# Splitting every pair of hidden chunks: low parts of 1+elu on GpSimd, an excess taken from each output tile, middle results in SBUF

## The chip, the cores and the metric

The kernel runs on one core of one Trainium2 chip. The metric is the device time of one execution in microseconds; before the change it is 1710.24 us, the median of three runs (1710.19 to 1712.89). The engines are called as the profile calls them: PE (TensorE), with PEld for its weight loads, DVE (VectorE), ACT (ScalarE), POOL (GpSimd) and SP (SyncE, which here issues DMAs). PE writes its results to PSUM; the other tiles lie in SBUF. L680 is line 680 of the kernel before.

## The reference

```python
def mab(q, kv):
    s = scale * (q @ kv.transpose(0, 2, 1))
    s = s - s.max(-1, keepdims=True)
    a = np.exp(s)
    a /= a.sum(-1, keepdims=True) + 1e-09
    return a @ kv
h = mab(I, x)                  # I: 32 inducing points, x: (4, 12480, 128)
attn = mab(x, h)               # (4, 12480, 128)

h = attn.reshape(49920, 128) @ w_in             # w_in: (128, 2048)
g = np.where(h > 0, h, np.exp(np.minimum(h, 0.0)) - 1.0)     # elu
out = g @ w_out                                 # w_out: (2048, 128)
```

Two attentions through 32 inducing points, then a feed-forward layer with 2048 hidden values per token and elu between its two products. Nearly all the work is the feed-forward layer. The weights are handed over as 64-bit floats, which the kernel takes apart itself; everything else is 32-bit.

## The kernel before

**Tiles.** The 12480 tokens of a batch are cut into 25 blocks, 15 of 512 tokens and 10 of 480, so there are 100 blocks (60 and 40) in four batches. The 2048 hidden values are 16 chunks of 128, taken two at a time: 8 pairs per block, 800 pairs in all. A tile of a pair is 128 partitions by 2 x 512 (or 2 x 480) values. Output stays transposed on the chip: a block's output tile is 128 output features by its tokens in one PSUM bank (`po`, two banks in turn), accumulated over all 8 pairs, and turned by DVE's transpose in squares of 32 by 32 (L688) before four DMAs on SP write it out.

**First product.** The second attention's weights a (32 per token) are not multiplied with h and then with w_in. h is multiplied with w_in once per batch (`project_h`), and the 32 rows of the result are stacked in a 128-row operand `hw` as high, low and high part and a block of ones; the attention weights are stacked for each block (`stk`) as high, high, low, and 1/32. One matmul per chunk (L618) in the type fp32r then gives ph = 1 + (attn @ w_in): the products of the parts, and the last 32 rows the one.

**One pair.** With ph = 1 + z in PSUM, four steps make the operands of the second product:

- `ffn_in` (L612): two matmuls into ph (three buffers `ph` of two banks), then ACT writes e = exp(ph - 1) into SBUF (L626, five buffers).
- `ffn_mid` (L629): DVE takes min(max(ph, 1), e), which is 1 + elu(z). For D pairs it goes back into ph in PSUM, for others into e in SBUF (L632).
- `ffn_split` (L636): for P and D pairs ACT writes gh, which is the value less one, rounded to fp32r (L641, four buffers).
- `ffn_low` (L643): what the rounding left, gl (four buffers). For D pairs DVE takes (ph - 1) - gh in one instruction (L648). For P and N pairs POOL first takes one from e in place (L653); for P pairs it then takes e - gh (L658).

The plan "PDNPDPND" (L28) says how each of the 8 pairs of a block is treated: three P, three D, two N. `ffn_out` (L660) does the second product into po (L680): for an N pair two matmuls in full 32-bit floats with the unsplit weights `wo_n`, which the profile shows as four instructions; for a split pair six matmuls in fp32r, gh with the high part `wo_h` of the weights, gh with their low part `wo_l`, and gl with `wo_h`, for each of two chunks.

**Order.** The order of the instructions on PE, DVE and ACT is written out by hand (L829 to L857). In round n come: the first product and exponential of pair n, the middle step and split of pair n-1, the low part of pair n-2, pieces of side work that have come due, and the second product of pair n-5 (LAG, L85; less at the beginning). So ACT's order is exponential n, split n-1; DVE's is middle step n-1, D low part n-2. Each engine takes its instructions in that order. POOL and SP are ordered by the framework.

**Side work.** The attention of later blocks and the next batch's first attention are cut into steps with due times (`attend` L699, `first_half` L707) and put between the pairs: scores on PE (L312, L531), transposes and reductions on DVE (L259, L394, L541, L549, L562, L579), exponentials on ACT, and on POOL the subtraction of the maximum (L550), the multiplication by the reciprocal sum (L570) and a low part (L591). The first batch's attention and the taking apart of the weights come before and among the first 13 pairs, in the hand-written order FIRST (L35): letters A to E are the stages of eight pieces of weights. L198, L202 and L208 are DVE's instructions in them, L212 and `split_w_out` (L230 to L239) make the final weights on POOL and ACT.

Of the kernel before, what the change touches and what calls it, by code (L numbers as in the profile page):

```python
# [9 lines left out]
F32 = mybir.dt.float32  # L10
F32R = mybir.dt.float32r
I32 = mybir.dt.int32
U32 = mybir.dt.uint32
AF = mybir.ActivationFunctionType
ALU = mybir.AluOpType
AX = mybir.AxisListType

P = 128
Q = 32
TM = 512  # L20
# [4 lines left out]

PLAN = "PDNPDPND"  # L28

# [13 lines left out]
def kernel(  # L45
# [8 lines left out]
    nc = tc.nc  # L54
    B, N, C = x.shape
# [18 lines left out]
    NFC = F // P  # L74
    NCP = NFC // 2
    assert len(PLAN) == NCP
    CHUNKS_S = [f for f in range(NFC) if PLAN[f // 2] != "N"]
    CHUNKS_N = [f for f in range(NFC) if PLAN[f // 2] == "N"]
    WHERE_S = {f: i for i, f in enumerate(CHUNKS_S)}
    WHERE_N = {f: i for i, f in enumerate(CHUNKS_N)}  # L80
    NSPLIT = len(CHUNKS_S)
    SCALE = 1.0 / math.sqrt(C)
    EPS = 1e-9

# [8 lines left out]
    const = ctx.enter_context(tc.tile_pool(name="const", bufs=1))  # L93
# [4 lines left out]
    ep = ctx.enter_context(tc.tile_pool(name="ep", bufs=2))  # L98
# [5 lines left out]
    ghp = ctx.enter_context(tc.tile_pool(name="ghp", bufs=GHB))  # L104
    glp = ctx.enter_context(tc.tile_pool(name="glp", bufs=GLB))
    op = ctx.enter_context(tc.tile_pool(name="op", bufs=2))
# [8 lines left out]
    def bank(name, take=False):  # L115
        if not steady and not take:
            return ps_h.tile([P, 2, 512], F32, tag="ph", name=name)[:, 0]
        t = ps_o.tile([P, 512], F32, tag=f"po{turn[0] % 2}", name=name)
        if take:
            turn[0] += 1  # L120
        return t
# [6 lines left out]
        out=fold, in_=ident.rearrange("p (c m) -> p m c", m=Q), axis=AX.X, op=ALU.add  # L128
    )
    sel4 = const.tile([P, 4, Q], F32, name="sel4")  # L130
    for c in range(4):
# [6 lines left out]
        out=mine, in_=ident.rearrange("p (c m) -> p c m", m=Q), axis=AX.X, op=ALU.add  # L138
# [5 lines left out]
    ps = bank("ps_ind")  # L144
# [3 lines left out]


    win_sb = const.tile([C, F], F32, name="win_sb")  # L150
    wo_n = const.tile([P, len(CHUNKS_N), C], F32, name="wo_n")
    wo_h = const.tile([P, NSPLIT, C], F32R, name="wo_h")
    wo_l = const.tile([P, NSPLIT, C], F32R, name="wo_l")
    WS = 512
    rebias = const.tile([P, 1], F32, name="rebias")
    nc.gpsimd.memset(rebias, -896.0)
# [73 lines left out]
    def split_w_out(s, w):  # L230
        for i in range(WC):
            f = s * WC + i
            t = w.low[:, i * C : (i + 1) * C]
            if f in WHERE_N:
                nc.scalar.copy(wo_n[:, WHERE_N[f], :], t)
            if f in WHERE_S:
                n = WHERE_S[f]
                nc.scalar.copy(wo_h[:, n, :], t)  # L238
                nc.gpsimd.tensor_sub(wo_l[:, n, :], t, wo_h[:, n, :].bitcast(F32))  # L239


    xT = {}
# [363 lines left out]
    live = {}  # L606

    def plan(n):
        b, k, cp = units[n]
        return PLAN[cp]  # L610

# [16 lines left out]

    def ffn_mid(n):  # L629
        v = live[n]  # L630
        v["g"] = v["ph"] if plan(n) == "D" else v["e"]
        nc.vector.scalar_tensor_tensor(  # L632
            out=v["g"], in0=v["ph"], scalar=1.0, in1=v["e"], op0=ALU.max, op1=ALU.min
        )

    def ffn_split(n):  # L636
        v, how = live[n], plan(n)
        shape = list(v["e"].shape)
        if how != "N":
            v["gh"] = ghp.tile(shape, F32R, tag="gh", name=f"gh_{n}")  # L640
            nc.scalar.activation(v["gh"], v["g"], AF.Copy, bias=-1.0)  # L641

    def ffn_low(n):  # L643
        v, how = live[n], plan(n)
        shape = list(v["e"].shape)
        if how == "D":
            v["gl"] = glp.tile(shape, F32R, tag="gl", name=f"gl_{n}")
            nc.vector.scalar_tensor_tensor(  # L648
                out=v["gl"], in0=v["g"], scalar=-1.0, in1=v["gh"].bitcast(F32),
                op0=ALU.add, op1=ALU.subtract,  # L650
            )
        else:
            nc.gpsimd.tensor_scalar(  # L653
                out=v["e"], in0=v["e"], scalar1=-1.0, scalar2=1.0, op0=ALU.add, op1=ALU.mult
            )
        if how == "P":
            v["gl"] = glp.tile(shape, F32R, tag="gl", name=f"gl_{n}")
            nc.gpsimd.tensor_sub(v["gl"], v["e"], v["gh"].bitcast(F32))  # L658

    def ffn_out(n):  # L660
        b, k, cp = units[n]
        v, how = live.pop(n), plan(n)
        T = BLOCKS[k][1]
        U = T // Q
        if cp == 0:
            outs[b, k] = bank(f"po_{b}_{k}", take=True)
        po = outs[b, k]
        parts = []
        for i in range(2):
            f = 2 * cp + i  # L670
            if how == "N":
                parts.append((0, wo_n[:, WHERE_N[f], :], v["e"][:, i]))
            else:
                w = WHERE_S[f]
                parts.append((1, wo_h[:, w, :], v["gh"][:, i]))
                parts.append((1, wo_l[:, w, :], v["gh"][:, i]))
                parts.append((2, wo_h[:, w, :], v["gl"][:, i]))
        parts.sort(key=lambda v: v[0])
        for i, (_, w, g) in enumerate(parts):
            nc.tensor.matmul(  # L680
                po[:, :T], w, g,
                start=(cp == 0 and i == 0),
                stop=(cp == NCP - 1 and i == len(parts) - 1),
            )
        if cp == NCP - 1:
            yield 1
            o = op.tile([P, U, Q], F32, tag="o", name=f"o_{b}_{k}")
            nc.vector.transpose(o.rearrange("p u d -> p (u d)"), po[:, :T])  # L688
            at = b * N + BLOCKS[k][0]
            dst = out[at : at + T, :]  # L690
            for dq in range(4):
                nc.sync.dma_start(
                    dst[:, dq * Q : (dq + 1) * Q].rearrange("(u t) d -> t u d", t=Q),
                    o[dq * Q : (dq + 1) * Q, :, :],
                )
# [45 lines left out]
    def first_batch(b):  # L741
# [32 lines left out]
        for s, w in enumerate(win + [w for w, _ in wout]):  # L774
            steps[f"A{s}"], steps[f"C{s}"] = w.take_apart, w.put_together
            steps[f"B{s}"] = lambda w=w, s=s: w.scale_of(s >= 6)
            if s < len(win):
                steps[f"D{s}"] = lambda w=w, s=s: w.finish(win_sb[:, s * WS : (s + 1) * WS])
            else:
                steps[f"D{s}"] = w.finish  # L780
                steps[f"E{s}"] = lambda w=w, s=s: split_w_out(s - len(win), w)
# [47 lines left out]
    for n, (b, k, cp) in enumerate(units):  # L829
        ffn_in(n)  # L830
        if n >= 1:
            ffn_mid(n - 1)
            ffn_split(n - 1)
        if n >= 2:
            ffn_low(n - 2)
        for r in list(running):
            go_on(r, n)
        while rest and rest[0][0] != f"u{n + 1}":
            step = rest.pop(0)[1]
            if step:  # L840
                step()
        if not rest:
            steady.append(True)
        while done <= n - min(LAG, RAMP + n // 4):
            begin(n, lambda: ffn_out(done))
            done += 1
        while side and side[0][0] <= n / NCP:
            begin(n, *side.pop(0)[1:])
    last = len(units)
    ffn_mid(last - 1)  # L850
    ffn_split(last - 1)
    ffn_low(last - 2)
    ffn_low(last - 1)
    for n in range(done, last):
        begin(last + n, lambda: ffn_out(n))
        for r in list(running):
            go_on(r, last + n + 1)  # L857
# [32 lines left out]
```

## Time and profile before

| | before |
|---|---|
| runs, median (lowest to highest) | 1710.24 us (1710.19 to 1712.89) |
| span of the profiled execution | 1710.8 us |
| PE busy | 1656.3 us, 97% |
| DVE busy | 1522.5 us, 89% |
| ACT busy | 1390.6 us, 81% |
| POOL busy | 1342.3 us, 78% |
| granted PE clock, mean | 0.986 |
| DMA, mean | 57 GB/s |

The profiled execution's own time is read from its span, the time from its first to its last instruction, 1710.8 us; it stands beside the runs' 1710.24. In a group's row come line, engine, operation, output and input tiles with shapes, and count; then the busy time of the group in us and the mean length of one instruction in ns; then how long its engine had been idle just before such instructions and who ended that. A row of the timeline gives start and length in us, engine, line, and in brackets idle time before it and who ended it. Instructions of one engine overlap at their ends, so lengths add up to more than the time that they take; starts are the safer measure. A row by stretch gives the length of the stretch, then the busy time of PE, PEld, DVE, ACT and POOL with counts, the granted clock, the DMA share and GB/s.

### The profile page before, as it was taken

What the parts mean: (1) busy time and instruction counts of PE and PEld (TensorE: products, weight loads), DVE (VectorE), ACT (ScalarE), POOL (GpSimd) and SP (SyncE); (2) the same over time, 40 slices, a digit from 0 to 9 for tenths busy, and PEclk for the clock granted to TensorE, in tenths of its full rate; (3) what the DMA queues carried; (4) which work ended last, traced back from release to release, by engine and by line L of the source; (5) the groups of instructions that cost most, each with busy time, mean ns of one, the idle gap of its engine ahead of it and who ended that gap; (6) DMA issues with size and microseconds to landing.
All of it is one profiled execution on the core that took longest, in us unless ns stands there. A gap on an engine that the chain in (4) does not pass through costs nothing.

```text
span 1710.8 us, 22335 instructions
## 1 busy us (share of the span) xinstructions
PE 1656.3 (97%) x7448; PEld 1176.5 (69%) x7448; DVE 1522.5 (89%) x1575; ACT 1390.6 (81%) x1620; POOL 1342.3 (78%) x948
## 2 busy tenths in 40 slices
PE   6589999999999999999999999999999999999998
PEld 4356776677776776767776676677777677777776
DVE  5799899898899998988989999889888989998996
ACT  4378888888787888888888888888878888888886
POOL 4488787787797877877888787787778888888886
PEclk9699999999999999999999999999999999999999
DMA  7144223322324233232223332321222111111111
GB/s 249 35 91 80 56 43 78 63 48 70 70 46 83 37 75 70 45 62 58 71 64 54 65 62 53 75 55 21 74 49 40 35 20 36 28 37 19 36 25 19
DMA packets 384754, 98.10 MB, mean 57 GB/s; under 512 B 364864, under 2 KB 370784, under 8 KB 384384
## 3 DMA queue, kind: packets, MB, share of 16 engines
q1 hardware_dynamic: 384640, 96.68, 27.9%
q8 instruction: 59, 0.97, 0.2%
q14 instruction: 55, 0.45, 0.1%
HBM read 48.94 MB, written 25.56 MB: 44 GB/s over the span
## 4 chain that ended last, share of the span: by engine, by line
PE 87%; DVE 7%; ACT 3%; issue 2%; DMA 1%; POOL 0%; SPq 0%; DVEq 0%; ACTq 0%
PE po L680 62%; PE ph L618 20%; ACT e L626 2%; DVE e L632 1%; PE ps_s L312 1%; PE ps_t L531 1%; PE ps_hh L403 1%; DVE ph L632 1%; ACT gh L641 1%; DMA xm<-in_x_dram 1%; DVE o L688 1%; DVE w_part L198 1%; DVE gl L648 0%; DMA w_raw<-in_moe_w_in_dram 0%; PE ps_hw L467 0%
## 5 line engine op out<-in xcount | busy, mean ns | idle before, releaser
L626 ACT ACTIVATE e<-ph 128x1024 f32<-128x1024 f32 (+1 forms) x800 | 803.4, 1005 | 228.8 <-PE ph L618 223.7
L653 POOL TENSOR_SCALAR e<-e 128x1024 f32<-128x1024 f32 (+1 forms) x500 | 510.8, 1029 | 280.6 <-ACT gh L641 270.4
L658 POOL TENSOR_TENSOR gl<-e,gh 128x1024 fp32r<-128x1024 f32 (+1 forms) x300 | 703.8, 2346 | 16.8
L632 DVE SCALAR_TENSOR_TENSOR e<-ph,e 128x1024 f32<-128x1024 f32 (+1 forms) x500 | 594.5, 1189 | 88.0 <-ACT e L626 84.9
L618 PE MATMUL ph<-stk,hw 128*128 128x512 f32 (+1 forms) x1600 | 566.8, 436 | 15.8 <-DVE e L632 9.6
L680 PE MATMUL po<-gh,wo_h 128*128 128x512 f32 (+1 forms) x1200 | 469.2, 391 | 7.5 <-ACT wo_h L238 3.5
L680 PE MATMUL po<-gh,wo_l 128*128 128x512 f32 (+1 forms) x1200 | 469.3, 391 | 6.6 <-POOL wo_l L239 6.6
L618 PEld LDWEIGHTS ph<-stk,hw 128*128 128x128 f32 x1600 | 295.4, 189 | 188.9 <-issue 84.9
L632 DVE SCALAR_TENSOR_TENSOR ph<-ph,e 128x1024 f32<-128x1024 f32 (+1 forms) x300 | 359.3, 1198 | 63.1 <-ACT e L626 62.3
L680 PE MATMUL po<-gl,wo_h 128*128 128x512 f32 (+1 forms) x1200 | 371.1, 390 | 0.7 <-POOL gl L658 0.7
L680 PE MATMUL po<-e,wo_n 128*128 128x512 f32 (+1 forms) x800 | 367.8, 582 | 0.1
L648 DVE SCALAR_TENSOR_TENSOR gl<-ph,gh 128x1024 fp32r<-128x1024 f32 (+1 forms) x300 | 356.3, 1188 | 1.0 <-ACT gh L641 1.0
L641 ACT ACTIVATE gh<-e 128x1024 fp32r<-128x1024 f32 (+1 forms) x300 | 311.3, 1038 | 13.9 <-DVE e L632 13.5
L641 ACT ACTIVATE gh<-ph 128x1024 fp32r<-128x1024 f32 (+1 forms) x300 | 300.6, 1002 | 19.1 <-DVE ph L632 18.2
L680 PEld LDWEIGHTS po<-gh,wo_h 128*128 128x128 f32 x1200 | 225.9, 188 | 56.6 <-issue 7.4
L680 PEld LDWEIGHTS po<-gh,wo_l 128*128 128x128 f32 x1200 | 225.9, 188 | 56.5 <-POOL wo_l L239 8.2
L680 PEld LDWEIGHTS po<-gl,wo_h 128*128 128x128 f32 x1200 | 225.6, 188 | 49.1 <-POOL gl L658 1.7
L680 PEld LDWEIGHTS po<-e,wo_n 128*128 128x128 f32 x800 | 150.6, 189 | 106.3 <-issue 91.3
L688 DVE STREAM_TRANSPOSE o<-po 128x512 f32<-128x512 f32 (+1 forms) x100 | 69.1, 691 | 4.0 <-PE po L680 4.0
L259 DVE STREAM_TRANSPOSE xT<-xq 128x1024 f32<-128x1024 f32 (+2 forms) x39 | 45.5, 1166 | 0.0
L570 POOL TENSOR_TENSOR s<-s,sm 128x512 f32<-128x512 f32 (+3 forms) x27 | 27.7, 1027 | 19.3 <-DVE sm L569 19.3
L403 PEld LDWEIGHTS ps_hh<-xm,e 128*32 128x32 f32 (+2 forms) x872 | 24.6, 115 | 16.9 <-issue 12.3
(99 smaller groups left out, 557.5 us busy)
## 6 DMA issues: line engine op xcount, KB each, us to landing
xm<-in_x_dram SPq DMA_DIRECT2D x32, 512.0 KB, 4.8
out_dram<-o SPq DMA_DIRECT2D x240, 64.0 KB, 2.0
xq<-in_x_dram SPq DMA_DIRECT2D x84, 128.0 KB, 2.9
out_dram<-o SPq DMA_DIRECT2D x160, 60.0 KB, 2.0
stk<-ahi SPq DMA_DIRECT2D x118, 64.0 KB, 2.0
xq<-in_x_dram SPq DMA_DIRECT2D x60, 120.0 KB, 2.8
stk<-ahi SPq DMA_DIRECT2D x80, 60.0 KB, 2.0
stk<-alo SPq DMA_DIRECT2D x59, 64.0 KB, 2.0
```

The lines of the kernel that those rows point to most:

```text
L259: nc.vector.transpose(t, xq.rearrange("p u d -> p (u d)"))
L403: nc.tensor.matmul(ps[c * Q : (c + 1) * Q, :C], st["e", g][:np_, u * Q : (u + 1) * Q], st["xm", g, u - u % UP][:np_, u % UP, :], start=(u ...
L570: eng.tensor_tensor(out=s, in0=s, in1=sm.unsqueeze(2).broadcast_to([np_, U, Q]), op=ALU.mult)
L618: nc.tensor.matmul(ph[:, i], state[b]["hw"][:, f * P : (f + 1) * P], stacks[b, k], start=True, stop=True,)
L626: nc.scalar.activation(e, ph, AF.Exp, bias=-1.0)
L632: nc.vector.scalar_tensor_tensor(out=v["g"], in0=v["ph"], scalar=1.0, in1=v["e"], op0=ALU.max, op1=ALU.min)
L641: nc.scalar.activation(v["gh"], v["g"], AF.Copy, bias=-1.0)
L648: nc.vector.scalar_tensor_tensor(out=v["gl"], in0=v["g"], scalar=-1.0, in1=v["gh"].bitcast(F32), op0=ALU.add, op1=ALU.subtract,)
L653: nc.gpsimd.tensor_scalar(out=v["e"], in0=v["e"], scalar1=-1.0, scalar2=1.0, op0=ALU.add, op1=ALU.mult)
L658: nc.gpsimd.tensor_sub(v["gl"], v["e"], v["gh"].bitcast(F32))
L680: nc.tensor.matmul(po[:, :T], w, g, start=(cp == 0 and i == 0), stop=(cp == NCP - 1 and i == len(parts) - 1),)
L688: nc.vector.transpose(o.rearrange("p u d -> p (u d)"), po[:, :T])
```

## The change

The plan becomes "PDPPDPDP": both N pairs become P pairs, so a block has five P and three D pairs, and all weights are split. For P pairs the split no longer takes one away: gh is 1 + elu rounded, gl what the rounding left, so POOL's minus-one (L653) is dropped for all pairs. The output then holds too much: for each output feature, the sum of the weights of the ten chunks of P pairs. That sum is made once, when the first block's last pair reaches its second product (`sum_excess`): six matmuls of ones with the split weights and four small DVE reductions. POOL subtracts it from every output tile after the transpose, in SBUF, and the output DMAs wait for that. The middle step writes into e, in SBUF, for all pairs; so the D pairs' split and low part read e where they read ph, and ph comes free after the middle step.

```diff
-PLAN = "PDNPDPND"
+PLAN = "PDPPDPDP"
...
-    wo_n = const.tile([P, len(CHUNKS_N), C], F32, name="wo_n")
-    wo_h = const.tile([P, NSPLIT, C], F32R, name="wo_h")
-    wo_l = const.tile([P, NSPLIT, C], F32R, name="wo_l")
+    wo_h = const.tile([P, NFC, C], F32R, name="wo_h")
+    wo_l = const.tile([P, NFC, C], F32R, name="wo_l")
+    excess = const.tile([P, Q], F32, name="excess")
...
     def ffn_mid(n):
         v = live[n]
-        v["g"] = v["ph"] if plan(n) == "D" else v["e"]
         nc.vector.scalar_tensor_tensor(
-            out=v["g"], in0=v["ph"], scalar=1.0, in1=v["e"], op0=ALU.max, op1=ALU.min
+            out=v["e"], in0=v.pop("ph"), scalar=1.0, in1=v["e"], op0=ALU.max, op1=ALU.min
         )
 
     def ffn_split(n):
...
+        v["gh"] = ghp.tile(list(v["e"].shape), F32R, tag="gh", name=f"gh_{n}")
+        nc.scalar.activation(
+            v["gh"], v["e"], AF.Copy, bias=0.0 if plan(n) == "P" else -1.0
+        )
 
     def ffn_low(n):
...
+        v["gl"] = glp.tile(list(v["e"].shape), F32R, tag="gl", name=f"gl_{n}")
+        gh = v["gh"].bitcast(F32)
+        if plan(n) == "P":
+            nc.gpsimd.tensor_sub(v["gl"], v["e"], gh)
+        else:
             nc.vector.scalar_tensor_tensor(
-                out=v["gl"], in0=v["g"], scalar=-1.0, in1=v["gh"].bitcast(F32),
-                op0=ALU.add, op1=ALU.subtract,
-            )
-        else:
-            nc.gpsimd.tensor_scalar(
-                out=v["e"], in0=v["e"], scalar1=-1.0, scalar2=1.0, op0=ALU.add, op1=ALU.mult
-            )
...
+                out=v["gl"], in0=v["e"], scalar=-1.0, in1=gh, op0=ALU.add, op1=ALU.subtract
+            )
+
+    def sum_excess():
+        ones = ep.tile([P, TM], F32, tag="e", name="ones")[:, :P]
+        ones_r = ones.bitcast(F32R)
+        nc.gpsimd.memset(ones, 1.0)
+        n_p = 2 * PLAN.count("P")
+        parts = [w[:, i : min(i + 4, n_p), :] for w in (wo_h, wo_l) for i in range(0, n_p, 4)]
+        ps = bank("ps_excess")
+        for i, w in enumerate(parts):
+            m = w.shape[1] * C
+            nc.tensor.matmul(
+                ps[:, :m], ones_r, w.rearrange("p c d -> p (c d)"),
+                start=i == 0, stop=i == len(parts) - 1,
+            )
+        for dq in range(4):
+            rows = slice(dq * Q, (dq + 1) * Q)
+            nc.vector.tensor_reduce(
+                out=excess[rows],
+                in_=ps.rearrange("p (c d) -> p d c", d=C)[rows, rows, :],
+                axis=AX.X, op=ALU.add,
+            )
...
+        if n == NCP - 1:
+            sum_excess()
...
             nc.vector.transpose(o.rearrange("p u d -> p (u d)"), po[:, :T])
+            nc.gpsimd.tensor_tensor(
+                out=o, in0=o, in1=excess.unsqueeze(1).broadcast_to([P, U, Q]), op=ALU.subtract
+            )
             at = b * N + BLOCKS[k][0]
```

The lines left out index the weights by one list for all chunks (P chunks first) and write the same six matmuls for every pair.

More of the change, by code (lines that the diff above doesn't have):

```diff
@@ L76 @@
     assert len(PLAN) == NCP
[L77 to L81, printed above, removed]
+    ORDER = [f for how in "PD" for f in range(NFC) if PLAN[f // 2] == how]
+    WHERE = {f: i for i, f in enumerate(ORDER)}
     SCALE = 1.0 / math.sqrt(C)
@@ L233, in split_w_out @@
             t = w.low[:, i * C : (i + 1) * C]
[L234 to L239, printed above, removed]
+            n = WHERE[f]
+            nc.scalar.copy(wo_h[:, n, :], t)
+            nc.gpsimd.tensor_sub(wo_l[:, n, :], t, wo_h[:, n, :].bitcast(F32))
     xT = {}
@@ L630, in ffn_mid @@
         v = live[n]
-        v["g"] = v["ph"] if plan(n) == "D" else v["e"]
         nc.vector.scalar_tensor_tensor(
-            out=v["g"], in0=v["ph"], scalar=1.0, in1=v["e"], op0=ALU.max, op1=ALU.min
+            out=v["e"], in0=v.pop("ph"), scalar=1.0, in1=v["e"], op0=ALU.max, op1=ALU.min
         )
     def ffn_split(n):
[L637 to L641, printed above, removed]
@@ L643, in ffn_low @@
-    def ffn_low(n):
[L644 to L647, printed above, removed]
+        v = live[n]
+        v["gh"] = ghp.tile(list(v["e"].shape), F32R, tag="gh", name=f"gh_{n}")
+        nc.scalar.activation(
+            v["gh"], v["e"], AF.Copy, bias=0.0 if plan(n) == "P" else -1.0
+        )
+    def ffn_low(n):
+        v = live[n]
+        v["gl"] = glp.tile(list(v["e"].shape), F32R, tag="gl", name=f"gl_{n}")
[3 more added lines that the diff above has]
+        else:
@@ L648, in ffn_low @@
             nc.vector.scalar_tensor_tensor(
-                out=v["gl"], in0=v["g"], scalar=-1.0, in1=v["gh"].bitcast(F32),
-                op0=ALU.add, op1=ALU.subtract,
-            )
-        else:
-            nc.gpsimd.tensor_scalar(
-                out=v["e"], in0=v["e"], scalar1=-1.0, scalar2=1.0, op0=ALU.add, op1=ALU.mult
-            )
-        if how == "P":
-            v["gl"] = glp.tile(shape, F32R, tag="gl", name=f"gl_{n}")
-            nc.gpsimd.tensor_sub(v["gl"], v["e"], v["gh"].bitcast(F32))
+                out=v["gl"], in0=v["e"], scalar=-1.0, in1=gh, op0=ALU.add, op1=ALU.subtract
+            )
@@ L660, in ffn_out @@
     def ffn_out(n):
         b, k, cp = units[n]
-        v, how = live.pop(n), plan(n)
+        v = live.pop(n)
         T = BLOCKS[k][1]
@@ L669, in ffn_out @@
         for i in range(2):
[L670 to L679, printed above, removed]
+            w = WHERE[2 * cp + i]
+            parts.append((wo_h[:, w, :], v["gh"][:, i]))
+            parts.append((wo_l[:, w, :], v["gh"][:, i]))
+        for i in range(2):
+            parts.append((wo_h[:, WHERE[2 * cp + i], :], v["gl"][:, i]))
+        if n == NCP - 1:
+            sum_excess()
+        for i, (w, g) in enumerate(parts):
             nc.tensor.matmul(
```

## The prediction

> **What bounds the kernel now.** I read the page's busy shares first, then the waits and the chain, then the busy times by stretch.
>
> ```profile
> span 1710.8 us, 22335 instructions
> PE 1656.3 (97%) x7448; PEld 1176.5 (69%) x7448; DVE 1522.5 (89%) x1575; ACT 1390.6 (81%) x1620; POOL 1342.3 (78%) x948
> PE 87%; DVE 7%; ACT 3%; issue 2%; DMA 1%; POOL 0%; SPq 0%; DVEq 0%; ACTq 0%
> L626 ACT ACTIVATE e<-ph 128x1024 f32<-128x1024 f32 (+1 forms) x800 | 803.4, 1005 | 228.8 <-PE ph L618 223.7
> ```
>
> ```profile
> 0.00:150.00 150.00, 107.95 (x640) 67.40 (x641) 118.76 (x165) 83.48 (x128) 90.61 (x89) 0.85 0.47 121
> 150.00:1698.00 1548.00, 1540.82 (x6781) 1103.81 (x6780) 1400.71 (x1408) 1306.01 (x1492) 1248.09 (x858) 1.00 0.26 51
> 1698.00:1711.00 13.00, 7.55 (x30) 5.28 (x28) 3.01 (x3) 1.11 (x2) 3.56 (x3) 0.90 0.12 19
> ```
>
> The last rows give, after the length, the busy time of PE, PEld, DVE, ACT and POOL. From 150 us on PE is busy 1541 of 1548 us, PE is 87% of the chain, and ACT's exponentials wait for PE: TensorE bounds the kernel. DVE idles 31 us before 150 us, 147 in the middle, 10 at the end. The span, 1710.8 us, stands 0.6 us above the median of the runs, so I add nothing for what lies around it, and all sums below are made against 1711.
>
> **TensorE: a gain.** These are PE's rows in the middle of the run: start, length, line.
>
> ```profile
> 1002.20 0.62 PE L618 MATMUL ph<-stk,hw 128*128 128x512 f32 x2
> 1002.66 1.88 PE L680 MATMUL po<-e,wo_n 128*128 128x512 f32 x4
> 1003.97 1.03 PE L618 MATMUL ph<-stk,hw 128*128 128x512 f32 x2
> 1004.84 0.39 PE L680 MATMUL po<-gh,wo_h 128*128 128x512 f32 x1
> ...
> 1006.24 0.62 PE L618 MATMUL ph<-stk,hw 128*128 128x512 f32 x2
> 1006.70 0.39 PE L680 MATMUL po<-gh,wo_h 128*128 128x512 f32 x1
> ```
>
> Matmuls overlap, so I count from start to start. An N pair with its first product is 1002.66 to 1004.84, 2.18 us; a split pair with the same is 1004.84 to 1006.70, 1.86. Each of 200 N pairs (2 of 8 in 100 blocks) saves 0.32 us, 0.31 in the mean with the 40 blocks of 480 tokens scaled by 480/512: 62 us. PE's 1656 becomes 1594. If nothing else came late, its 54 us of idle time would remain: 1648.
>
> **ScalarE: nearly the new bound.**
>
> ```profile
> 1465.30 1.05 ACT L641 ACTIVATE gh<-e 128x1024 fp32r<-128x1024 f32 x1
> 1466.25 1.02 ACT L626 ACTIVATE e<-ph 128x1024 f32<-128x1024 f32 x1
> 1467.15 1.03 ACT L641 ACTIVATE gh<-ph 128x1024 fp32r<-128x1024 f32 x1
> 1468.10 1.03 ACT L626 ACTIVATE e<-ph 128x1024 f32<-128x1024 f32 x1
> 1469.02 1.05 ACT L641 ACTIVATE gh<-e 128x1024 fp32r<-128x1024 f32 x1
> ```
>
> From start to start an exponential costs 0.91 us and a split 0.95, whether it reads SBUF or PSUM. 200 more splits of 0.95 (0.93 with the shorter blocks) add 186: 1577. A block of 512 tokens needs 8 x 1.87 = 14.96 us of ACT against 8 x 1.86 = 14.88 of PE; with ACT's 66 us of idle before 150 us and 12 in the tail this alone gives 1577 + 78 = 1655.
>
> **GpSimd.**
>
> ```profile
> L653 POOL TENSOR_SCALAR e<-e 128x1024 f32<-128x1024 f32 (+1 forms) x500 | 510.8, 1029 | 280.6 <-ACT gh L641 270.4
> L658 POOL TENSOR_TENSOR gl<-e,gh 128x1024 fp32r<-128x1024 f32 (+1 forms) x300 | 703.8, 2346 | 16.8
> L570 POOL TENSOR_TENSOR s<-s,sm 128x512 f32<-128x512 f32 (+3 forms) x27 | 27.7, 1027 | 19.3 <-DVE sm L569 19.3
> ```
>
> The 500 minus-ones go (-511), 200 low parts of 2.346 come (+469), and 100 subtractions of the excess from an output tile come: same size and broadcast as L570, 1.03 each, +103. POOL's sum is 1403. It has less to do per unit of time than ACT, but it will be at work most of the time, and that matters next.
>
> **VectorE: same instructions, one of them in another place.** The 300 D low parts now read both operands from SBUF; before, one was ph in PSUM. The trace shows few VectorE instructions with two SBUF operands, nearly all at the start. These are they, with the GpSimd work beside them, and a lone one for comparison.
>
> ```profile
> 86.30 0.69 DVE L198 SCALAR_TENSOR_TENSOR w_part<-w_raw,w_part 128x512 uint32<-128x512 uint32 x1 [1.11 <-POOL w_part L192]
> 96.81 2.69 DVE L198 SCALAR_TENSOR_TENSOR w_part<-w_raw,w_part 128x512 uint32<-128x512 uint32 x1
> ...
> 72.87 1.46 DVE L570 TENSOR_TENSOR s<-s,sm 96x512 f32<-96x512 f32 x1
> 74.25 2.83 DVE L198 SCALAR_TENSOR_TENSOR w_part<-w_raw,w_part 128x512 uint32<-128x512 uint32 x1
> ```
>
> ```profile
> 72.50 1.28 POOL L212 TENSOR_TENSOR w_raw<-w_raw,w_part 128x512 f32<-128x512 f32 x1
> 73.75 2.79 POOL L658 TENSOR_TENSOR gl<-e,gh 128x1024 fp32r<-128x1024 f32 x1
> 76.50 0.90 POOL L239 TENSOR_TENSOR wo_l<-w_raw,wo_h 128x128 fp32r<-128x128 f32 x1
> ...
> 96.61 2.34 POOL L658 TENSOR_TENSOR gl<-e,gh 128x1024 fp32r<-128x1024 f32 x1
> ```
>
> L198 takes 0.69 us alone. Issued at 96.81, behind a GpSimd low part that runs to 98.95, it ends at 99.50, 0.55 after that. At 72.87 L570 ends 0.55 after POOL's L212; the POOL low part of 73.75 ends 2.21 after L570. At 74.25 L198 ends 0.54 after that low part, and POOL's next instruction, queued right behind, did not get in first. So the two exclude each other: VectorE waits out GpSimd's running instruction, then takes 0.14 us less than alone, and GpSimd's next loses in turn. The middle step (one operand in PSUM) shows nothing of this:
>
> ```profile
> L632 DVE SCALAR_TENSOR_TENSOR e<-ph,e x466: 1095/1206/1226, 199.1 to 1696.8; 128x1024 f32<-128x1024 f32 x89, 128x960 f32<-128x960 f32 x67
> L431 DVE SCALAR_TENSOR_TENSOR es<-es,scale,es x5: 218/734/1236, 47.8 to 1257.9; 128x1 f32<-128x1 f32 x5
> ```
>
> The columns are minimum, median, maximum in ns: L632 never strays over 500 POOL low parts and minus-ones, while the one-element L431, two SBUF operands, goes from 218 to 1236.
>
> I walk one block of 512 through this. Per pair ACT issues exponential, then the split of the pair before; DVE issues the middle step, then the D low part of the pair before; POOL its P low parts. Start-to-start on DVE:
>
> ```profile
> 1006.16 1.23 DVE L632 SCALAR_TENSOR_TENSOR e<-ph,e 128x1024 f32<-128x1024 f32 x1 [0.24 <-ACT e L626]
> 1007.30 1.21 DVE L648 SCALAR_TENSOR_TENSOR gl<-ph,gh 128x1024 fp32r<-128x1024 f32 x1
> 1008.44 0.70 DVE L579 STREAM_TRANSPOSE aT<-s 128x512 f32<-128x512 f32 x1
> ```
>
> ```profile
> L658 POOL TENSOR_TENSOR gl<-e,gh 128x1024 fp32r<-128x1024 f32 x180 | 432.4, 2402 | 9.9
> ```
>
> 1.13 for either; the groups by form give 2.40 for a POOL low part of this size. Count from the start of D's split, ACT at its pace of 1.87. The next exponential has ended at 0.11, its middle step is issued, and DVE reaches the D low part at 1.24. The middle step queued behind that must start by 2 x 1.87 - 1.22 = 2.52, or ACT's split two pairs on comes late; unhindered it starts at 2.37, so 0.15 is to spare. A D low part held until r lets it start at r + 0.99 (1.13 - 0.14). D after one P: POOL took up that P's low part when its split ended, 1.06 after its start, and runs to 1.06 + 2.40 - 1.87 = 1.59: wait 0.35, ACT loses 0.06. D after two Ps: two low parts run to 1.06 + 4.80 - 3.81 = 2.05: wait 0.81, next middle step at 3.04, loss 0.52. The third D (after D, P): the low part before it starts only behind the second D's (3.12) and the excess subtraction (0.84 more) and runs to 6.36; this D's split starts at 3.74 + 0.52 = 4.26 and its low part is ready at 5.32: wait 1.04, loss 0.57. Waits 2.20 less 3 x 0.14 is 1.78 per block, 0.59 per D low part; ACT's 14.96 becomes 16.11, against the 15.5 that two N pairs gave PE (2 x 2.18 + 6 x 1.86). VectorE, with eight middle steps (9.04), three low parts (5.17 with waits) and the output transpose (0.62), is then busy 14.8 of 16.11 before its attention work: it is the engine that bounds.
>
> So the sum goes by VectorE: 1522 + 300 x 0.59 x 0.97 (shorter blocks) = 1522 + 172 = 1694 of busy time; plus its idle: 31 at the start, 10 at the end, and half of the 1.3 us per block that the walk leaves (attention's transposes and reductions fill the rest), 65: 106. **1800 us.**
>
> Ends for the unknown wait: 0.35 on each (0.21 net, 61) with only the fixed 41 of idle gives 1522 + 61 + 41 = 1624, below the 1655 of ACT, so the low end there is ACT's; half a POOL low part on each, 1.20 (1.06 net, 308), with 65 to 106 of idle gives 1895 to 1936. I take 0.59 because the walk uses this order and these lengths.
>
> The Trainium skill, "SBUF — State Buffer", section "Who interferes with whom", has a rule against this change: a VectorE instruction with two SBUF inputs and a GpSimd one that reads SBUF lock each other out for the whole instruction. The rows agree but for 0.14 us of overlap; by the rule, with none, each D low part costs 0.14 more, 300 x 0.14 = 42: 1842. I stay with the rows.
>
> **The rest.** The sum of the excess is six matmuls of 0.23 and four small reductions, once; I allow 1 to 3 us at a point where ph tiles are already waited for, none of it on VectorE's account. Weight casts: four copies become four casts, with four more POOL subtractions like L239, 0.9 at most each, before POOL is needed. The output DMAs on SP now wait for POOL's subtraction (1 us, behind at most one or two low parts); behind them on SP are loads for much later, and the output tile has a second buffer. At the very end that chain costs one low part on POOL instead of DVE (+1.2) and one subtraction (+1.0): 2 us, covered by the rounding. Every gh now holds one of four buffers until its products ran, and in the walk those come over 2 us before the split that wants the buffer: nothing. Earlier release of ph by D pairs helps PE, which no longer bounds.
>
> **Rivals.** Faster, *the waits find slack*: should the low parts mostly fall between POOL's instructions, ACT's 1655 stands. Break-even, with 106 of idle, is 1711 = 1522 + 106 + 83: 0.29 net per D low part. For it: D never follows D, so POOL gets a gap after each. Against: POOL busy 1403 of 1655 is 85%. Chance 0.13.
> Slower still, *POOL falls behind*: five low parts, the subtraction and attention's own POOL work keep POOL always running, each D waits half of one: 1895 to 1936, about 1905. For it: POOL plus low parts, 1403 + 300 x 1.0, is already 1700. Against: DVE's delays slow POOL's supply too. Chance 0.15.
> *The gains and losses cancel* within 0.2% (3.4 us, what a measurement of this kernel can tell from no change): waits within 0.02 of break-even, 0.03.
>
> **How the numbers follow.** The forecast, 1800, has 0.69; its own range is 1735 (waits net of 0.4, 115 + 98 idle) to 1865 (net 0.8, 233 + 110 idle). Slower altogether 0.84, faster 0.13, same 0.03. For 8 in 10 the range goes on to the lower end of POOL falls behind: 1735 to 1895. Left out are faster and same, 0.16, and some 0.05 of the highest.
>
> **What would show it.** Right: D low parts (now of e and gh) at a mean of 1.6 to 2.0 us instead of 1.19, maximum beyond 3; POOL low parts up from 2.35 by some tenths; DVE at 94% or more; ACT's splits waiting for the middle step; PE's share below 92%, its pairs all of 1.86. Wrong: D low parts that stay at 1.2, and ACT or PE at 95%.

## The result, and the profile after

The changed kernel takes 1895.1 us, median of four runs (1893.15 to 1897.11), against 1710.22 before: ratio 1.1076, 95% interval 1.1061 to 1.1092. The forecast was 1800, range 1735 to 1895; the direction was right, the time ended 95 us above the forecast and just outside the range.

From the page of the changed kernel, the span, the engines' busy times, the chain's shares by engine, and the groups that answer to those of before:

```profile
span 1894.4 us, 24417 instructions
PE 1683.3 (89%) x7854; PEld 1269.2 (67%) x7854; DVE 1745.6 (92%) x1579; ACT 1580.1 (83%) x1820; POOL 1555.2 (82%) x753
DVE 36%; PE 29%; issue 16%; ACT 12%; POOL 4%; DMA 3%; SPq 0%; ACTq 0%; DVEq 0%; POOLq 0%
L641 POOL TENSOR_TENSOR gl<-e,gh 128x1024 fp32r<-128x1024 f32 (+1 forms) x500 | 1192.1, 2392 | 285.0 <-ACT gh L632 227.2
L625 DVE SCALAR_TENSOR_TENSOR e<-ph,e 128x1024 f32<-128x1024 f32 (+1 forms) x800 | 936.3, 1182 | 96.1 <-ACT e L620 93.2
L632 ACT ACTIVATE gh<-e 128x1024 fp32r<-128x1024 f32 (+1 forms) x800 | 828.8, 1036 | 225.3 <-DVE e L625 198.3
L620 ACT ACTIVATE e<-ph 128x1024 f32<-128x1024 f32 (+1 forms) x800 | 796.6, 996 | 29.6 <-PE ph L612 29.0
L612 PE MATMUL ph<-stk,hw 128*128 128x512 f32 (+1 forms) x1600 | 529.5, 413 | 117.7 <-DVE e L625 109.5
L643 DVE SCALAR_TENSOR_TENSOR gl<-e,gh 128x1024 fp32r<-128x1024 f32 (+1 forms) x300 | 576.3, 1921 | 10.0 <-ACT gh L632 6.0
L695 POOL TENSOR_TENSOR o<-o,excess 128x512 f32<-128x512 f32 (+1 forms) x100 | 198.7, 1987 | 1.6 <-DVE o L694 1.6
```

Lines have moved: L625 is now the middle step, L632 the split, L641 GpSimd's and L643 VectorE's low part, L695 the subtraction. VectorE's low part was this in the kernel before:

```profile
L648 DVE SCALAR_TENSOR_TENSOR gl<-ph,gh 128x1024 fp32r<-128x1024 f32 (+1 forms) x300 | 356.3, 1188 | 1.0 <-ACT gh L641 1.0
```

It went from 1.19 to 1.92 us; the middle step, with one operand in PSUM, stayed near 1.19, at 1.18. ACT, which before waited for PE, now waits 198 us for the middle step, and so does PE, 110 us: VectorE has become what the others wait for.

The low parts one by one, minimum, median and maximum in ns, in the changed kernel:

```profile
L643 DVE SCALAR_TENSOR_TENSOR gl<-e,gh x300: 1142/1620/6104, 81.8 to 1882.9; 128x1024 fp32r<-128x1024 f32 x90, 128x960 fp32r<-128x960 f32 x60
```

The trace says when they are slow. The 29 that were issued while GpSimd ran nothing took at most 1.23 us; nearly all of the other 271 end 1.0 to 1.1 us after an instruction of GpSimd's. But the maximum, 6.10, is longer than a wait for one such instruction, 2.4 us, can make it. The timeline of the changed kernel around one of these, VectorE first, then GpSimd, then ACT:

```profile
717.54 0.69 DVE L694 STREAM_TRANSPOSE o<-po 128x512 f32<-128x512 f32 x1
718.48 1.23 DVE L625 SCALAR_TENSOR_TENSOR e<-ph,e 128x1024 f32<-128x1024 f32 x1 [0.25 <-ACT e L620]
719.62 5.79 DVE L643 SCALAR_TENSOR_TENSOR gl<-e,gh 128x1024 fp32r<-128x1024 f32 x1
725.34 2.34 DVE L625 SCALAR_TENSOR_TENSOR e<-ph,e 128x1024 f32<-128x1024 f32 x2
```

```profile
718.37 2.41 POOL L641 TENSOR_TENSOR gl<-e,gh 128x1024 fp32r<-128x1024 f32 x1
720.75 1.28 POOL L695 TENSOR_TENSOR o<-o,excess 128x512 f32<-128x512 f32 x1
721.99 2.34 POOL L641 TENSOR_TENSOR gl<-e,gh 128x1024 fp32r<-128x1024 f32 x1
```

```profile
721.15 1.02 ACT L620 ACTIVATE e<-ph 128x1024 f32<-128x1024 f32 x1
726.64 1.06 ACT L632 ACTIVATE gh<-e 128x1024 fp32r<-128x1024 f32 x1 [4.47 <-DVE e L625]
```

VectorE's low part is issued at 719.62, while a GpSimd low part runs to 720.78. By the prediction's rule it was next. Instead the subtraction and one more low part run first, and it ends at 725.41, 1.08 after the last of them. Behind it wait the middle step, and behind that ACT, 4.5 us. Of the 300 low parts 11 took 5.5 us or more, 64.8 us together; the other 289 have a mean of 1.77.

### The profile page after: what moved, and what is told of

It reads as the page before. It is cut to its first block, busy times and chain, and to the rows that moved or that the text cites. A ratio compares the mean times of both kernels' runs of the same rounds, so it can differ in the third digit from the quotient of the medians.

```text
span 1894.4 us, 24417 instructions
## 1 busy us (share of the span) xinstructions
PE 1683.3 (89%) x7854; PEld 1269.2 (67%) x7854; DVE 1745.6 (92%) x1579; ACT 1580.1 (83%) x1820; POOL 1555.2 (82%) x753
## 4 chain that ended last, share of the span: by engine, by line
DVE 36%; PE 29%; issue 16%; ACT 12%; POOL 4%; DMA 3%; SPq 0%; ACTq 0%; DVEq 0%; POOLq 0%
PE po L686 19%; DVE gl L643 17%; DVE e L625 13%; PE ph L612 7%; ACT e L620 6%; ACT gh L632 6%; POOL gl L641 2%; DMA xm<-in_x_dram 1%; DVE o L694 1%; DVE xT L253 1%; POOL o L695 1%; PE ps_t L525 1%; PE ps_s L306 1%; DVE e L388 1%; DMA stk<-ahi 1%
## 5 line engine op out<-in xcount | busy, mean ns | idle before, releaser
L641 POOL TENSOR_TENSOR gl<-e,gh 128x1024 fp32r<-128x1024 f32 (+1 forms) x500 | 1192.1, 2392 | 285.0 <-ACT gh L632 227.2
L625 DVE SCALAR_TENSOR_TENSOR e<-ph,e 128x1024 f32<-128x1024 f32 (+1 forms) x800 | 936.3, 1182 | 96.1 <-ACT e L620 93.2
L632 ACT ACTIVATE gh<-e 128x1024 fp32r<-128x1024 f32 (+1 forms) x800 | 828.8, 1036 | 225.3 <-DVE e L625 198.3
L686 PE MATMUL po<-gh,wo_h 128*128 128x512 f32 (+1 forms) x1600 | 640.4, 400 | 38.6 <-DVE s L535 12.5
L686 PE MATMUL po<-gh,wo_l 128*128 128x512 f32 (+1 forms) x1600 | 636.8, 398 | 2.3 <-POOL wo_l L233 2.3
L643 DVE SCALAR_TENSOR_TENSOR gl<-e,gh 128x1024 fp32r<-128x1024 f32 (+1 forms) x300 | 576.3, 1921 | 10.0 <-ACT gh L632 6.0
L686 PE MATMUL po<-gl,wo_h 128*128 128x512 f32 (+1 forms) x1600 | 503.2, 396 | 4.3 <-POOL gl L641 4.2
L686 PEld LDWEIGHTS po<-gh,wo_h 128*128 128x128 f32 x1600 | 308.4, 193 | 116.0 <-ACT e L620 20.8
L686 PEld LDWEIGHTS po<-gh,wo_l 128*128 128x128 f32 x1600 | 308.9, 193 | 66.6 <-POOL wo_l L233 5.0
L695 POOL TENSOR_TENSOR o<-o,excess 128x512 f32<-128x512 f32 (+1 forms) x100 | 198.7, 1987 | 1.6 <-DVE o L694 1.6
```

What stands on the lines that cost most here:

```text
L625: nc.vector.scalar_tensor_tensor(out=v["e"], in0=v.pop("ph"), scalar=1.0, in1=v["e"], op0=ALU.max, op1=ALU.min)
L632: nc.scalar.activation(v["gh"], v["e"], AF.Copy, bias=0.0 if plan(n) == "P" else -1.0)
L641: nc.gpsimd.tensor_sub(v["gl"], v["e"], gh)
L643: nc.vector.scalar_tensor_tensor(out=v["gl"], in0=v["e"], scalar=-1.0, in1=gh, op0=ALU.add, op1=ALU.subtract)
L686: nc.tensor.matmul(po[:, :T], w, g, start=(cp == 0 and i == 0), stop=(cp == NCP - 1 and i == len(parts) - 1),)
L695: nc.gpsimd.tensor_tensor(out=o, in0=o, in1=excess.unsqueeze(1).broadcast_to([P, U, Q]), op=ALU.subtract)
```

## The experiments

**The place alone, both ways.** The first undoes the place in the changed kernel, the second makes that change alone in the kernel before.

```diff
     def ffn_mid(n):                                # after_psum, from the changed kernel
         v = live[n]
+        v["g"] = v["ph"] if plan(n) == "D" else v["e"]
...
-            out=v["e"], in0=v.pop("ph"), scalar=1.0, in1=v["e"], op0=ALU.max, op1=ALU.min
+            out=v["g"], in0=v["ph"], scalar=1.0, in1=v["e"], op0=ALU.max, op1=ALU.min
...
-            v["gh"], v["e"], AF.Copy, bias=0.0 if plan(n) == "P" else -1.0
+            v["gh"], v["g"], AF.Copy, bias=0.0 if plan(n) == "P" else -1.0
...
-                out=v["gl"], in0=v["e"], scalar=-1.0, in1=gh, op0=ALU.add, op1=ALU.subtract
+                out=v["gl"], in0=v["g"], scalar=-1.0, in1=gh, op0=ALU.add, op1=ALU.subtract
```

> The changed kernel with one thing undone: the D pairs' middle step goes back into ph in PSUM, and their split and low part read it there. Theory (the D low part of two SBUF operands and GpSimd's low parts lock each other out): the D low part is back at 1.19 us from 1.92, GpSimd's excess subtraction at 1.03 from 1.99, ACT becomes the bound, 1655 to 1690 us, faster than before. Rival (the added work on ACT and GpSimd costs the time, the place of the operand does not): the time stays above 1850.

```diff
-        v["g"] = v["ph"] if plan(n) == "D" else v["e"]      # before_sbuf, from the kernel before
+        v["g"] = v["e"]
```

> The kernel before with that one part of the change alone: the D pairs' middle step goes into e in SBUF. Theory: the D low part goes from 1.19 to 1.6 to 2.0 us and the time from 1710 to 1760 to 1860, with no split or low part added. Rival (added work): 1710 within 5 us, the D low part at 1.2.

after_psum took 1701.74 us (ratio to the kernel before 0.9945, 0.9928 to 0.9961), before_sbuf 1838.01 (1.0743, 1.0727 to 1.0759). The groups of after_psum, then of before_sbuf:

```profile
PE 1616.8 (95%) x7854; PEld 1243.6 (73%) x7854; DVE 1526.9 (90%) x1579; ACT 1558.4 (92%) x1820; POOL 1426.6 (84%) x753
L644 DVE SCALAR_TENSOR_TENSOR gl<-ph,gh 128x1024 fp32r<-128x1024 f32 (+1 forms) x300 | 356.1, 1187 | 3.7 <-ACT gh L633 3.5
L696 POOL TENSOR_TENSOR o<-o,excess 128x512 f32<-128x512 f32 (+1 forms) x100 | 127.5, 1275 | 2.6 <-DVE o L695 2.6
```

```profile
DVE 74%; ACT 9%; issue 6%; PE 5%; POOL 3%; DMA 2%; SPq 1%; DVEq 0%; POOLq 0%; ACTq 0%
L648 DVE SCALAR_TENSOR_TENSOR gl<-e,gh 128x1024 fp32r<-128x1024 f32 (+1 forms) x300 | 609.9, 2033 | 1.5 <-ACT gh L641 1.1
```

This settles the main cause. One operand moved back takes 193 us off the changed kernel; the same operand moved in the kernel before costs 127 us with no split, no low part and no subtraction added, and hands the chain to VectorE. The added work, with what it saves PE, makes the kernel no slower: after_psum is 9 us, or half a per cent, below the kernel before. But it misses the theory's 1655 to 1690. PE's busy time falls by 40 us, from 1656 to 1617, and not by the 62 of the forecast, and its idle time rises from 54 to 83. With PE at 95%, ACT at 92% and VectorE at 90%, no single engine holds the chain of after_psum:

```profile
PE 46%; ACT 22%; DVE 14%; issue 12%; POOL 2%; DMA 2%; SPq 0%; DVEq 0%; ACTq 0%; POOLq 0%
```

**What GpSimd does meanwhile.** Two runs change the other side of the collision.

```diff
-            nc.gpsimd.tensor_tensor(                 # after_no_subtraction
-                out=o, in0=o, in1=excess.unsqueeze(1).broadcast_to([P, U, Q]), op=ALU.subtract
-            )
```

> The changed kernel without GpSimd's subtraction of the excess, which is left out, so that the output keeps it. Theory: the subtraction makes one D low part in three wait longer; without it the D low part's mean falls from 1.92 to 1.6 to 1.8 us and the time by 20 to 70 us, to 1825 to 1875. Rival (GpSimd's total work sets the time): its 199 us of busy time come off whole, about 1700.

```diff
-            nc.gpsimd.tensor_sub(v["gl"], v["e"], gh)     # after_pool_writes_only
+            nc.gpsimd.memset(v["gl"].bitcast(F32), 0.0)
```

> The changed kernel with GpSimd's low parts replaced by filling gl with zero, so that GpSimd still writes as much but reads nothing there (the low parts of P pairs are left out of the result). Theory (what collides is reading): the D low part is at 1.19 to 1.3 us, the time 1655 to 1700. Rival (writing collides as well, or the D low part is slow by itself with two SBUF operands): the D low part stays above 1.5 us.

Without the subtraction 1803.89 us (1.0544, 1.0528 to 1.0559): 91 us less, more than the theory had said and less than half of the rival's 199. With GpSimd only filling, 1681.79 (0.9829, 0.9810 to 0.9849), inside the theory's range. The busy times and low parts of the first, then of the second:

```profile
PE 1642.6 (91%) x7854; PEld 1255.6 (70%) x7854; DVE 1660.6 (92%) x1579; ACT 1576.3 (88%) x1820; POOL 1373.3 (76%) x653
L643 DVE SCALAR_TENSOR_TENSOR gl<-e,gh x300: 1142/1490/2787, 79.3 to 1791.6; 128x1024 fp32r<-128x1024 f32 x90, 128x960 fp32r<-128x960 f32 x60
```

```profile
L641 POOL MEMSET gl<- 128x1024 f32 (+1 forms) x500 | 467.4, 935 | 693.1 <-PE po L686 685.6
L643 DVE SCALAR_TENSOR_TENSOR gl<-e,gh 128x1024 fp32r<-128x1024 f32 (+1 forms) x300 | 367.2, 1224 | 5.2 <-ACT gh L632 4.1
```

So two operands in SBUF are not slow by themselves: 1.22 us beside a GpSimd that writes 500 tiles there and reads little. (It is also busy for less time, 739 us against 1555, so writing alone was not tried at the same load. But the 168 low parts beside which GpSimd did nothing but fill took at most 1.23 us each; the maximum of all, 1.44, lies beside a subtraction.) The middle step's result lies in SBUF here as in the changed kernel, so neither the split's reading it there nor the earlier release of ph is what costs the time. And the maximum without the subtraction is 2.8 us: the low parts of 5.5 us and more came only with it here. VectorE's busy time fell by 85 of the 91 us.

The same subtraction where no low part can be held up:

```diff
-            nc.gpsimd.tensor_tensor(                 # after_psum_no_subtraction, from after_psum
-                out=o, in0=o, in1=excess.unsqueeze(1).broadcast_to([P, U, Q]), op=ALU.subtract
-            )
```

> after_psum without GpSimd's subtraction of the excess, which is left out, so that the output keeps it. Theory (the 91 us that the subtraction costs in the changed kernel are the lockout's, not GpSimd's work): without a low part that it can hold up it costs 0 to 12 us, 1690 to 1702. Rival (it is its 127 us of GpSimd work, or the output DMAs that wait for it): 60 us or more come off, 1640 or less.

1700.41 us (0.9944, 0.9929 to 0.9959), 1.3 below after_psum. The subtraction and the output DMAs behind it are free there; its 91 us in the changed kernel are the collision's.

**Why VectorE is passed over.** Two runs looked for what makes the longest low parts.

```diff
-PLAN = "PDPPDPDP"      # after_order
+PLAN = "DPDPPDPP"
```

> The changed kernel with the same five P and three D pairs in another order, DPDPPDPP: the excess subtraction now stands on GpSimd's queue between the low parts of two P pairs, when no D low part is waiting. Theory (in the changed kernel 11 D low parts of 300 took 5.6 to 6.1 us, since the subtraction and the low part behind it went ahead of the waiting VectorE, and most of what lies above the forecast follows from them): the longest D low part is under 3.5 us, the time 1815 to 1860. Rival (it is GpSimd's load, wherever the subtraction stands): D low parts of about 6 us remain, 1875 to 1910.

```diff
-                out=o, in0=o, in1=excess.unsqueeze(1).broadcast_to([P, U, Q]), op=ALU.subtract   # after_square
+                out=o, in0=o, in1=o, op=ALU.mult
```

> The changed kernel with GpSimd's subtraction replaced by the output tile times itself, so that the output is squared and keeps the excess: as many elements in two SBUF inputs, but without the repeated 32 values of the excess. The D low parts of 5.6 to 6.1 us come where VectorE does not get its turn beside GpSimd. If the repeated operand makes it so, the longest D low part is below 3.5 us and the time 1820 to 1870; if any short two-input instruction there does it, some of about 6 us remain, at 1875 to 1910.

after_order took 1918.32 us (1.1211, 1.1196 to 1.1226), above the rival's range too: the theory fell. Its low parts were shorter in the mean, 1.84, and VectorE's busy time was 31 us below the changed kernel's, but 8 low parts still took 5.4 us or more. They are issued while the subtraction runs, and both GpSimd low parts behind it go first. The timeline of after_order, VectorE and then GpSimd:

```profile
725.28 6.18 DVE L643 SCALAR_TENSOR_TENSOR gl<-e,gh 128x1024 fp32r<-128x1024 f32 x1
```

```profile
724.42 1.29 POOL L695 TENSOR_TENSOR o<-o,excess 128x512 f32<-128x512 f32 x1
725.68 4.69 POOL L641 TENSOR_TENSOR gl<-e,gh 128x1024 fp32r<-128x1024 f32 x2
```

The order costs time in another way: VectorE idles 201 us there, 152 of it ahead of middle steps that wait for ACT's exponentials. Why ACT is late in this order is open.

```profile
L625 DVE SCALAR_TENSOR_TENSOR e<-ph,e 128x1024 f32<-128x1024 f32 (+1 forms) x800 | 936.0, 1180 | 153.1 <-ACT e L620 151.8
```

after_square took 1858.46 us (1.0864, 1.0833 to 1.0896). The answers are mixed: the time lies where the repeated operand was to be the cause, but 8 low parts took over 5 us, so it is not the reason that VectorE is passed over. The square is also a shorter instruction, 1.04 us against the subtraction's 1.29 when nothing holds them up, and this quarter of a microsecond, where VectorE waits, is part of the 37 us between the two. That length is not the repeated operand's either: in the kernel before, a GpSimd subtraction with two full tiles of the same size takes 1.30.

```profile
L591 POOL TENSOR_TENSOR alo<-aT,ahi 128x512 fp32r<-128x512 f32 x11 | 14.3, 1297 | 0.7 <-ACT ahi L589 0.7
```

**Slack in the order.** The last run of the changed kernel gave the middle step more time.

```diff
         if n >= 1:                       # after_late_split
             ffn_mid(n - 1)
-            ffn_split(n - 1)
         if n >= 2:
-            ffn_low(n - 2)
+            ffn_split(n - 2)
+        if n >= 3:
+            ffn_low(n - 3)
...
```

> The changed kernel with every split and low part issued one round later (split of pair n-2 and low part of n-3 in round n), so that a middle step held up by a D low part has one more exponential and split, 1.87 us, before ACT misses it. Theory (beside the waits themselves the time goes into ACT, DVE and PE waiting for each other in turn, as the order leaves 0.15 us to spare): ACT's 198 us of waiting for the middle step fall below 80 and the time to 1800 to 1850. Rival (GpSimd and VectorE have no more to give between them, whatever the order): 1870 or more, the waiting found elsewhere.

1910.02 us (1.1158, 1.1139 to 1.1177): the rival's side. ACT's waiting for the middle step is gone, as the theory had it, but not the time:

```profile
L620 ACT ACTIVATE e<-ph 128x1024 f32<-128x1024 f32 (+1 forms) x800 | 807.0, 1009 | 275.7 <-PE ph L612 145.3
L632 ACT ACTIVATE gh<-e 128x1024 fp32r<-128x1024 f32 (+1 forms) x800 | 834.9, 1044 | 3.9 <-DVE e L625 3.6
L643 DVE SCALAR_TENSOR_TENSOR gl<-e,gh 128x1024 fp32r<-128x1024 f32 (+1 forms) x300 | 604.0, 2013 | 0.0
```

It has moved to the exponential, which waits 145 us for PE (itself 93 us behind GpSimd's low parts), and 112 us for VectorE's low parts themselves, which hold e's five buffers a round longer. Here 14 low parts took over 5 us, some between two GpSimd low parts with no subtraction near, so the subtraction isn't a necessary part of it. As the buffers stayed at five, this run does not tell what the order alone is worth.

**One pair fewer for ACT and GpSimd.** From after_psum, one P pair becomes N again, in the new way: its 1 + elu goes unsplit into full 32-bit matmuls, and its weights into the excess.

```diff
-PLAN = "PDPPDPDP"      # after_psum_one_n, from after_psum
+PLAN = "PDNPDPDP"
...
+        if plan(n) == "N":           # in ffn_split and ffn_low
+            return
...
+            if w >= NSPLIT:          # in ffn_out
+                parts.append((wo_n[:, w - NSPLIT, :], v["e"][:, i]))
+                continue
...
+        nc.tensor.matmul(ps[:, : (NFC - NSPLIT) * C], ones, sum_n, start=False, stop=True)
```

> after_psum with one P pair of eight treated as N again (plan PDNPDPDP): no split, no low part, 1+elu in full 32-bit floats, and its weights in the excess. If ACT and GpSimd together are what keeps after_psum at 1702 (ACT 92%, PE 95%), then 100 splits and 100 POOL low parts less, for 32 us more of PE, give 1675 to 1695. If PE is already what bounds after_psum, 1715 to 1735.

1701.33 us (0.9946, 0.9934 to 0.9959), between the two answers and level with after_psum:

```profile
PE 1634.5 (96%) x7654; PEld 1212.6 (71%) x7654; DVE 1526.5 (90%) x1579; ACT 1476.8 (87%) x1720; POOL 1193.3 (70%) x651
PE 76%; DVE 9%; ACT 8%; issue 4%; DMA 1%; POOL 1%; SPq 0%; POOLq 0%; DVEq 0%; ACTq 0%
```

82 us less of ACT and 233 less of GpSimd bought what 18 us more of PE (the expectation had 32) cost. PE again has three quarters of the chain. Of the kernels here that leave nothing out, after_psum and this one are the fastest.

## Why the prediction was right and wrong

**The collision, right.** That VectorE's low part and GpSimd's instructions exclude each other once both of its operands lie in SBUF was read from a few rows of the startup, and after_psum and before_sbuf show it: 1.19 us with one operand in PSUM, 1.92 and 2.03 without. The middle step is untouched, 1.18. Two of the signs that were to show it missed: VectorE was busy 92% and not 94, and GpSimd's own low parts went from 2.35 to 2.39 us only and not up by some tenths. GpSimd's loss lies in the subtraction, 1.99 us here against 1.28 in after_psum.

**The engines' sums, right for ACT and GpSimd, too low for PE.** ACT was to be busy 1577 us and is 1580. A split pair takes PE 1.86 us where nothing holds it up, here from 1005.88 to 1007.74, in PE's rows of the changed kernel:

```profile
1005.88 0.62 PE L612 MATMUL ph<-stk,hw 128*128 128x512 f32 x2
1006.34 0.39 PE L686 MATMUL po<-gh,wo_h 128*128 128x512 f32 x1
...
1007.74 0.62 PE L612 MATMUL ph<-stk,hw 128*128 128x512 f32 x2
```

But PE's sum was to be 1594 us and is 1683, and 1617 in after_psum. The halved clock, described at the end, is a part of the 1683: the mean granted clock is 0.960 here, 0.986 before and 0.988 in after_psum. What makes the 23 us in after_psum is not shown. GpSimd's 1403 us is 1427 where nothing collides (after_psum): the subtraction takes 1.275, not the 1.03 of the row that stood for it, L570. That instruction repeats its small operand along the other axis, so it was not the same broadcast.

**The sum by VectorE, wrong in both terms.** Forecast: 1694 busy and 106 idle, 1800. Measured: 1746 busy, and 149 idle in a span of 1894.

The step of the first that failed is "VectorE waits out GpSimd's running instruction", with its turn next. I had it from two places of the trace before, where GpSimd's next did not get in first. It holds for the most part: the 289 low parts below 5 us have a mean of 1.77, and the walk's value was 1.19 + 0.59 = 1.78. It fails for 11, each passed over by two GpSimd instructions: 64.8 us where 11 x 1.77 = 19 were counted, 45 of the 52 that the first term lacks. (Three more were passed over by the subtraction alone and took 2.97.) That the walk hit 1.77 is partly luck. It took the subtraction too short; and done again without the subtraction it gives, as an estimate from its own numbers, the third D a wait of at most 3.12 + 2.40 - 5.32 = 0.20, and so a low part at most 1.19 + 0.31 = 1.50 in the mean. In after_no_subtraction the mean was 1.65.

The second term's step is "half of the 1.3 us per block that the walk leaves", the idle time of VectorE beside attention's work. It is too small even where no low part takes over 2.8 us: without the subtraction VectorE idles 1801.0 - 1660.6 = 140 us. The walk held one block's pairs only, with ACT never early nor late by anything but the low part; in the kernel VectorE waits for exponentials (93 us) that ACT could not issue, because it stood at a split that waited for VectorE. That this loop makes the difference of 43 us is argued from the waits; after_late_split, made to show it, moved the waiting into other buffers and leaves it open.

**The rivals.** *POOL falls behind* names the measured time, 1895 to 1936, but not for its reason: it has every low part wait 1.20, and the mean wait was 1.92 - 1.19 + 0.14 = 0.87; GpSimd stood idle 285 us ahead of its low parts. *The waits find slack* was priced too well at 1655: where the collision is taken away, the kernel takes 1682 (GpSimd only filling) or 1702 (operand in PSUM). ACT's 1577 and its fixed idle time were not all: in after_psum ACT is busy 1558 us and idle 142, PE 1617 and 83. That their stalls do not lie in the same places is argued, not shown.

**The rest.** The output DMAs, the sum of the excess and the weight casts were put at nothing to 3 us. after_psum_no_subtraction bears out the DMAs; PE's weight loads waited 7.8 us for the casts' high parts where it was 4.2. The sum of the excess was to take nothing of VectorE, which stood 3.5 us waiting for its matmuls. The buffers of gh were put at nothing too: ACT's splits stood 19.8 us waiting for products.

## What to carry to other kernels

Where VectorE and GpSimd are both at work most of the time, count the SBUF tensor inputs of each VectorE instruction. In this kernel a second input that stayed in PSUM was worth 193 us, though it held its PSUM buffer longer. Such a change can be judged from the few instructions of the startup that already have the operands in question, by comparing their lengths beside GpSimd and alone. And where two engines exclude each other, do not count on taking turns: price some cases of being passed over, and price the waits of every engine in the loop, not only those of the one that collides.

## What the runs showed of the hardware

VectorE does not always get its turn. Low parts of over 5 us, with one or two queued GpSimd instructions run ahead of the waiting VectorE, came 11 times in 300 in the changed kernel, 8 times in after_order and in after_square, 14 in after_late_split, and never in after_no_subtraction (maximum 2.8 us) or before_sbuf (3.3). Neither the place of the subtraction nor its repeated operand decides it; what does is open.

Filling on GpSimd does not hold VectorE up (at most 1.23 us beside fills alone). The Trainium skill, "SBUF — State Buffer", section "Who interferes with whom", says that a GpSimd instruction that only writes does not contend with two SBUF inputs; this agrees, at GpSimd's lower load.

A long wait costs PE twice. In the changed kernel PE's clock, the third figure from the end in these rows by stretch, falls after it stood for 4.3 us behind the low part of 719.62:

```profile
721.00:726.00 5.00, 1.30 (x6) 0.72 (x4) 5.00 (x2) 1.17 (x2) 3.33 (x2) 1.00 0.34 52
726.00:728.00 2.00, 1.40 (x3) 1.16 (x4) 1.95 (x3) 1.36 (x2) 0.00 (x0) 0.50 0.00 0
728.00:730.00 2.00, 2.00 (x7) 1.58 (x6) 2.00 (x2) 2.00 (x3) 0.37 (x1) 0.64 0.00 0
730.00:732.00 2.00, 2.00 (x10) 1.60 (x10) 1.81 (x3) 2.00 (x3) 2.00 (x2) 1.00 0.00 0
```

The matmuls after it follow each other at 0.43 us until 729.3, and then at 0.23 again:

```profile
726.60 1.22 PE L612 MATMUL ph<-stk,hw 128*128 128x512 f32 x2 [4.30 <-DVE e L625]
...
728.05 0.63 PE L686 MATMUL po<-gh,wo_l 128*128 128x512 f32 x1
728.48 0.63 PE L686 MATMUL po<-gh,wo_h 128*128 128x512 f32 x1
...
730.30 0.39 PE L686 MATMUL po<-gh,wo_h 128*128 128x512 f32 x1
730.53 0.39 PE L686 MATMUL po<-gh,wo_l 128*128 128x512 f32 x1
```

The Trainium skill, "TensorE: Matmul & The Clock Gate", section "Part 1: The HAM clock gate", has the clock fall to half after an idle window of about 3.4 us; the trace agrees with that here.
